# Gradient of wo: four 1 MB stores over 128 partitions against 64 stores over 8 partitions each

## Chip, cores and metric

The kernel runs on one core of one Trainium2 chip. The metric is the device time of one execution in microseconds (us): median of three runs 1698.76, from 1698.05 to 1699.05. The profile is of one further execution, taken by the hardware profiler. All engine times below are counted from the first instruction of that execution. PE is the matmul engine, ACT, DVE and POOL the other three compute engines, and SP the engine that only issues transfers here. Sixteen DMA engines move the data between HBM and the on-chip memory.

## What is computed

Forward and backward of one transformer block at decode: four batch rows, one new token each, width 512, 32 heads of 128, cached keys and values of 4096 positions per head, and a gated feed-forward layer of width 1792.

```python
def _A_ref(x, k_cache, v_cache, wq, wo):
    q = (x @ wq).reshape(B, Sq, H, Dh).transpose(0, 2, 1, 3)
    scores = jnp.einsum("bhqd,bhkd->bhqk", q, k_cache) * (Dh ** -0.5)
    p = _softmax(scores, axis=-1)
    o = jnp.einsum("bhqk,bhkd->bhqd", p, v_cache)
    return o.transpose(0, 2, 1, 3).reshape(B, Sq, H * Dh) @ wo
...
h = x + _A_ref(_layernorm(x, axis=-1), A_k_cache, A_v_cache, A_wq, A_wo)
h2 = h + _B_ref(_layernorm(h, axis=-1), B_w1, B_w3, B_w2)
```

The outputs are `h2` and the gradients of x, k_cache, v_cache, wq, wo, w1, w3 and w2, all bf16. The caches are 128 heads (batch times head) of 4096 x 128 each, 1 MB a head: K is read once, V twice, and both gradients, `out_2` for K and `out_3` for V, are written once. That is most of the 707 MB moved. The gradient of wo, `out_5`, is 4096 x 512: for every batch row an outer product of the attention output (4096 wide) and the gradient at the block's output (512 wide), summed over the four rows. It is 4 MB.

## The kernel before

The program is written with an explicit order of instructions for each engine (a manual schedule); a framework puts the semaphores between them. On-chip memory is one arena of 23 slots of some 8 KB per partition. `Slot` takes one slot, `Slot2` a pair of neighbours, and `give` returns it when the last user has been issued, not when it is done; the next user of the slot then waits on semaphores. Which free slot is taken follows from how long ago, in program order, each was given back.

The work goes in three stages. In the first, to about 650 us, K and V are read head by head, and scores, softmax and per-head sums are formed. The second, short, does the feed-forward layer. The third reads V again and writes the gradients of both caches. It begins one head at a time (`for s in range(SP)`, SP = 32 heads) and then goes over pairs of heads: `for t in range(NT)`, 48 passes, each with these steps in this order:

- `load_pairs(t + LP)` (L1280): SP issues the load of one 2 MB pair of V, some passes ahead;
- `front_pair(t + LP, ...)`: PE transposes the eight parts of a V pair (L1298), ACT copies them back (L1299), PE forms the products for dP (L1313). In its middle stands a call of `side`;
- `more_V`: DVE makes the 2 MB gradient of a V pair as an outer product (L1379), SP stores it to `out_3` (L1389). How far V's gradients run ahead of K's shrinks near the end, and a pass in which it shrinks makes none;
- `grad_pair(out_2, ...)`: the same two lines for the gradient of K; after every second pass `group_dS_pair` (L1326, L1329) prepares the next two;
- `side(s + 1)`.

`side` moves the small work forward: a generator, `side_work`, that holds everything which isn't a gradient of the caches. In this loop each call of `side` takes two steps, from one `yield` to the next, so a pass has four. A step is mostly one `grad_unit`: a matmul (L984) into one of two PSUM buffers named `gps`, and the copy by ACT of the unit before (L978). The last part of `side_work` is the gradient of wo, L1139 to L1148: four blocks of 1024 rows, each made of eight units in a slot over 128 partitions (eight rows of `out_5`, 8 KB, in each partition) and stored by one transfer on SP (L1146). After the last of them the flag `side_done` lets the pairs take any slots.

SP issues its transfers in program order and waits, before each, for what the transfer needs. Everything that moves in bulk goes through its one queue. At the end of the program SP waits for all transfers (L1519).

Of the kernel before, what the change touches and what calls it, by code (L numbers as in the profile page):

```python
# [27 lines left out]
def kernel(  # L28
# [22 lines left out]
    nc = tc.nc  # L51
    P = nc.NUM_PARTITIONS

    B = A_x.shape[0]
    D = A_x.shape[-1]
    H = A_k_cache.shape[1]
# [4 lines left out]
    HD = H * Dh  # L61
# [152 lines left out]
    def ones_window(col):  # L214
# [11 lines left out]
                          in_=rowg[:, None, :, None].to_broadcast([P, 4, 8, 4]))  # L226
# [70 lines left out]
    with ExitStack() as c0:  # L297
# [11 lines left out]
        for h in range(H):  # L309
            for cc in range(DC):  # L310
                nc.tensor.matmul(qT_ps[:, h, :], lhsT=wq_s[cc].b(HD)[:, h * Dh:(h + 1) * Dh], rhs=xhatT[:, cc, :],
                                 start=(cc == 0), stop=(cc == DC - 1))
# [4 lines left out]
        for r in range(2):  # L317
            for t_ in range(2):
                for q in range(4):
                    nc.tensor.matmul(qr_ps[32 * q:32 * (q + 1), 2 * r + t_, :], lhsT=ident_b[:, 64 * r + t_:64 * (r + 1):2],  # L320
                                     rhs=qT_bf[:], start=True, stop=True, tile_position=(0, 32 * q))
# [514 lines left out]
    with ExitStack() as cm:  # L836
# [33 lines left out]
        for wi, wt in enumerate((w1, w3)):  # L870
            for fc in range(FC):
                for cc in range(DC):
                    nc.tensor.matmul(gu_ps[:, wi, fc, :], lhsT=w13_view(wt, cc)[:, fc * P:(fc + 1) * P], rhs=hhatT[:, cc, :],  # L873
                                     start=(cc == 0), stop=(cc == DC - 1))
# [25 lines left out]
        for jj in range(DC):  # L900
            i_mm = 0
            for (lt, wt) in ((d_gateT_bf, w1), (d_upT_bf, w3)):
                for fc in range(FC):
                    nc.tensor.matmul(dn_ps[:, jj, :], lhsT=w13_view(wt, jj)[:, fc * P:(fc + 1) * P], rhs=lt[:, fc, :],  # L904
                                     start=(i_mm == 0), stop=(i_mm == 2 * FC - 1))
# [12 lines left out]
        ps = psA.tile([P, REP, Dh], FP32, tag="rT", name="repq_ps")  # L918
# [4 lines left out]
        for s in range(3):  # L923
# [8 lines left out]
                         start=True, stop=True)  # L932
# [14 lines left out]
        for b0, b1 in ((0, 1), (1, B)):  # L947
            ps = psA.tile([P, B, Dh], FP32, tag="rT", name="rep_ps")
            for b in range(b0, b1):
                for jj in range(DC):  # L950
                    nc.tensor.matmul(ps[:, b, :], lhsT=dhT[:, jj, b:b + 1].to_broadcast([P, P]), rhs=wo_page(0)[:, 0, jj, :],
                                     start=(jj == 0), stop=(jj == DC - 1))
# [12 lines left out]
    with ExitStack() as c2:  # L965
# [9 lines left out]
        def grad_flush():  # L975
            if gu:
                dst, ps, n = gu.pop()
                nc.scalar.copy(out=dst, in_=ps[:, 0:n])  # L978


        def grad_unit(dst, lhsT, rhs):
            n = rhs.shape[-1]
            ps = psg.tile([P, 512], FP32, tag="gps", name="gps")
            nc.tensor.matmul(ps[:, 0:n], lhsT=lhsT, rhs=rhs, start=True, stop=True)  # L984
            grad_flush()
            gu.append((dst, ps, n))

# [22 lines left out]
        def side_work():  # L1010
# [22 lines left out]
            for cc in range(DC):  # L1033
# [9 lines left out]
                for h in range(H):  # L1043
                    nc.tensor.matmul(dx_ps[0:B, cc * P:(cc + 1) * P], lhsT=dqT_bf[:, h * B:(h + 1) * B], rhs=wv[:, h, :],
                                     start=(h == 0), stop=(h == H - 1))
# [19 lines left out]
            for cc in range(DC):  # L1065
                st = Slot("gwq")
                for n8 in range(HD // 512):
                    grad_unit(st.b(HD)[:, n8 * 512:(n8 + 1) * 512], xhat_bf[0:B, cc * P:(cc + 1) * P],
                              flat.b(HD)[0:B, n8 * 512:(n8 + 1) * 512])
                    yield  # L1070
                grad_flush()
                nc.sync.dma_start(out=out_4[cc * P:(cc + 1) * P, :], in_=st.b(HD))
                if cc == DC - 1:
                    flat.give()
                    fs.give()
                st.give()
# [5 lines left out]
            gr_bf, dh_bf, hhat_bf = r1.t[0:B, 2 * F:2 * F + D], r2.t[0:B, F:F + D], r2.t[0:B, F + D:F + 2 * D]  # L1082
# [29 lines left out]
            for i in range(2):  # L1112
                st = Slot("gw2")
                hw = hh_rows[:, i * 7 * P:(i + 1) * 7 * P].rearrange("b (p k) -> b k p", k=7)
                for k in range(7):
                    grad_unit(st.b(7 * D)[:, k * D:(k + 1) * D], hw[:, k, :], gr_bf)
                    yield
                grad_flush()
                nc.sync.dma_start(out=out_8[i * 7 * P:(i + 1) * 7 * P, :].rearrange("(p c) j -> p c j", c=7),
                                  in_=st.b(7 * D).rearrange("p (c j) -> p c j", c=7))  # L1120
                st.give()
            oflat = Slot("oflat")
            for b in range(B):
                nc.gpsimd.dma_start(out=oflat.b(HD)[b:b + 1, :], in_=O_sb[b::B, :])
            for (rows, out_ap) in ((dg_rows, out_6), (du_rows, out_7)):
                for i in range(2):
                    st = Slot("gw13")
                    nw = hhat_bf[0:B, i * 2 * P:(i + 1) * 2 * P].rearrange("b (p k) -> b k p", k=2)
                    for k in range(2):
                        for (f0_, w_) in f_chunks:  # L1130
                            grad_unit(st.b(2 * F)[:, k * F + f0_:k * F + f0_ + w_],
                                      nw[:, k, :], rows[:, f0_:f0_ + w_])
                            yield
                    grad_flush()
                    nc.sync.dma_start(out=out_ap[i * 2 * P:(i + 1) * 2 * P, :].rearrange("(p c) f -> p c f", c=2),
                                      in_=st.b(2 * F).rearrange("p (c f) -> p c f", c=2))
                    st.give()
            r1.give()
            for h0 in range(0, H, 8):  # L1139
                st = Slot("gwo")  # L1140
                ow = oflat.b(HD)[0:B, h0 * P:(h0 + 8) * P].rearrange("b (p k) -> b k p", k=8)
                for k in range(8):
                    grad_unit(st.b(8 * D)[:, k * D:(k + 1) * D], ow[:, k, :], dh_bf)
                    yield
                grad_flush()
                nc.sync.dma_start(out=out_5[h0 * P:(h0 + 8) * P, :].rearrange("(p k) j -> p k j", k=8),  # L1146
                                  in_=st.b(8 * D).rearrange("p (k j) -> p k j", k=8))
                st.give()  # L1148
            oflat.give()
            r2.give()  # L1150
            part["side_done"] = True

        units["s"] = side_work()


# [368 lines left out]
```

## Time and profile before

| | |
|---|---|
| median of three runs | 1698.76 us |
| lowest and highest | 1698.05, 1699.05 us |
| span of the profiled execution, first to last instruction | 1696.2 us |
| median less that span | 2.6 us |
| busy: PE, DVE, ACT, POOL | 73%, 73%, 57%, 20% of the span |
| bytes moved by DMA | 707.45 MB, 417 GB/s over the span |
| SP's queue | 80416 packets, 704.94 MB |
| stores L1146 (gradient of wo) | 4 of 1 MB, issued from 1513.2 to 1610.4, landing 25.7 to 30.5 us later |
| stores L1389 (gradient pairs) | 96 of 2 MB, issued from 899.1 to 1666.8 |
| V pair loads L1280 | 48 of 2 MB, the last issued at 1610.8 |
| copies L978, 128x512 | 594 ns median |
| matmuls L984, four rows by 128 and 512 columns | 432 ns median |

The single execution that was profiled has no device time of its own beside its span; the table sets the span against the median. In the profile a row of slices gives the busy share in 40 equal parts of the span, one digit in tenths each. "Landing" is the time from the issue of a transfer to its last completion: each transfer reports 16 completions, and it has landed when all have come. In a list of waits, "A <- B" says that A waited for B, with the total in us, the number of times and the longest. In a timeline, a line gives the start and length of a run of like instructions, in us.

### The profile page before, as it was taken

The numbers are of one execution on the slowest core, as the hardware profiler recorded it, in microseconds if no ns is written. First come the engines' busy times: TensorE is split into PE (matmuls) and PEld (weight loads), VectorE is DVE, ScalarE is ACT, GpSimd is POOL, SyncE is SP. The second block draws the span as 40 slices with busy tenths as digits, with TensorE's granted clock in tenths as the row PEclk, the third lists the DMA queues.
The fourth block names the chain that finished last, engine by engine and source line by source line (L and its number), as shares of the span: only waits on it lengthen the run. The fifth ranks groups of instructions, "written<-read, shape, count | busy, mean of one in ns | idle before, by whom it ended". The sixth has DMA issues, their size and how long they took to land.

```text
span 1696.2 us, 37839 instructions
## 1 busy us (share of the span) xinstructions
PE 1233.4 (73%) x16228; PEld 943.4 (56%) x16228; DVE 1234.4 (73%) x1198; ACT 959.5 (57%) x1490; POOL 336.9 (20%) x583
## 2 busy tenths in 40 slices
PE   5889888888888888877876755667665666766650
PEld 4777667666677666655655544444444444444440
DVE  5989999999998997667766466575665655655683
ACT  3555544454454544677665555666665666666650
POOL 1211222222222222222231121011210102011120
PEclk8999999999999999899898689886678777676675
DMA  9999999999999999999999999999999999999995
GB/s 401 424 424 424 424 424 424 424 424 423 416 423 406 424 414 397 395 414 425 425 425 429 428 429 428 429 430 429 429 429 428 418 430 429 422 418 425 415 429 230
DMA packets 81000, 707.45 MB, mean 417 GB/s; under 512 B 8748, under 2 KB 12984, under 8 KB 15296
## 3 DMA queue, kind: packets, MB, share of 16 engines
q1 hardware_dynamic: 80416, 704.94, 99.0%
q8 instruction: 127, 2.08, 0.5%
q14 instruction: 41, 0.34, 0.0%
q0 software_dynamic: 416, 0.10, 0.0%
HBM read 422.59 MB, written 282.34 MB: 416 GB/s over the span
## 4 chain that ended last, share of the span: by engine, by line
DMA 46%; DVE 9%; PE 3%; issue 2%; ACT 1%; DVEq 0%; POOL 0%; SPq 0%; ACTq 0%
DMA out_dram<-arena 43%; DVE arena L1379 7%; DMA arena<-in_A_v_cache_dram 3%; DVE arena L806 1%; PE M_ps L472 1%; DVE arena L457 1%; PE pt_w L601 0%; ACT arena L1299 0%; ACT Pn L436 0%; DVEq L1519 0%; PE kP_ps L482 0%; DVE dPr L1326 0%; PE pt_tps L1298 0%; PE gu_ps L873 0%; PE dn_ps L904 0%
## 5 line engine op out<-in xcount | busy, mean ns | idle before, releaser
L1299 ACT COPY arena<-pt_tps 128x1024 bf16<-128x1024 bf16 x384 | 369.8, 1023 | 232.3 <-PE pt_tps L1298 231.6
L1298 PE MATMUL pt_tps<-ident_b,arena 128*128 128x128 bf16 x3072 | 308.1, 272 | 204.7 <-DMA arena<-in_A_v_cache_dram 149.4
L1298 PEld LDWEIGHTS <-arena 128*128 128x128 bf16 x3072 | 263.9, 125 | 304.2 <-DMA arena<-in_A_v_cache_dram 172.8
L1379 DVE TENSOR_TENSOR arena<-arena 128x8192 bf16<-128x8192 bf16 x48 | 212.5, 4427 | 205.1 <-DMA out_dram<-arena 202.3
L472 PE MATMUL M_ps<-arena 128*128 128x130 bf16 x4096 | 285.1, 222 | 42.9 <-DMA arena<-in_A_v_cache_dram 42.2
L457 DVE TENSOR_TENSOR arena<-arena 128x4096 bf16<-128x4096 bf16 x128 | 292.5, 2285 | 23.9 <-POOL arena L453 23.9
L472 PEld LDWEIGHTS <-arena 128*128 128x128 bf16 x4096 | 251.9, 99 | 64.0 <-DMA arena<-in_A_v_cache_dram 57.2
L1379 DVE TENSOR_TENSOR arena<-dS,arena 128x8192 bf16<-128x8192 bf16 x48 | 212.3, 4424 | 73.0 <-DMA out_dram<-arena 73.0
L364 DVE STREAM_TRANSPOSE arena<-arena 128x512 f32<-128x512 f32 (+1 forms) x321 | 250.7, 797 | 0.0
L359 ACT COPY arena<-pt_tps 128x1024 bf16<-128x1024 bf16 x128 | 129.5, 1012 | 188.9 <-PE pt_tps L358 150.5
L1376 POOL COPY arena<-arena 128x128 bf16<-128x128 bf16 x48 | 55.3, 1153 | 492.3 <-ACT arena L1353 286.3
L370 POOL TENSOR_TENSOR W<-qrep,wmask 128x128 bf16<-128x128 bf16 x128 | 120.2, 939 | 85.6 <-PE S_ps L390 70.8
L801 ACT COPY arena<-pt_tps 128x1024 bf16<-128x1024 bf16 x128 | 121.7, 1025 | 26.1 <-PE pt_tps L800 24.8
L453 POOL COPY arena<-P_all 128x64 bf16<-128x64 bf16 x128 | 32.7, 255 | 412.8 <-ACT P_all L447 409.8
L806 DVE TENSOR_TENSOR arena<-dS,arena 128x4096 bf16<-128x4096 bf16 x32 | 73.2, 2293 | 35.0 <-DMA out_dram<-arena 34.7
L800 PE MATMUL pt_tps<-ident_b,arena 128*128 128x128 bf16 x1024 | 78.5, 229 | 27.1 <-ACT arena L801 27.1
L1313 PE MATMUL dP_ps<-arena 128*32 128x512 bf16 x768 | 85.7, 484 | 7.6 <-ACT arena L1299 7.3
L800 PEld LDWEIGHTS <-arena 128*128 128x128 bf16 x1024 | 67.2, 104 | 37.5 <-issue 35.9
L447 ACT COPY P_all<-pt_P 32x64 bf16<-32x64 bf16 x256 | 52.1, 204 | 53.6 <-PE pt_P L443 51.4
L806 DVE TENSOR_TENSOR arena<-P,arena 128x4096 bf16<-128x4096 bf16 x29 | 66.4, 2295 | 19.8 <-DMA out_dram<-arena 19.8
L358 PE MATMUL pt_tps<-ident_b,arena 128*128 128x128 bf16 x1024 | 80.1, 222 | 0.0
L482 PE MATMUL kP_ps<-arena,onesw 128*32 128x512 bf16 x1024 | 79.6, 388 | 0.0
(245 smaller groups left out, 1576.5 us busy)
## 6 DMA issues: line engine op xcount, KB each, us to landing
out_dram<-arena SPq DMA_DIRECT2D x96, 2048.0 KB, 27.9
arena<-in_A_v_cache_dram SPq DMA_DIRECT2D x160, 1024.0 KB, 15.9
arena<-in_A_k_cache_dram SPq DMA_DIRECT2D x128, 1024.0 KB, 15.3
arena<-in_A_v_cache_dram SPq DMA_DIRECT2D x48, 2048.0 KB, 32.1
out_dram<-arena SPq DMA_DIRECT2D x72, 1024.0 KB, 20.2
arena<-in_A_wq_dram SPq DMA_DIRECT2D x8, 1024.0 KB, 14.4
arena<-in_B_w_dram SPq DMA_DIRECT2D x8, 896.0 KB, 15.3
out_dram<-arena SPq DMA_DIRECT2D x6, 896.0 KB, 28.4
```

The lines of the kernel that those rows point to most:

```text
L359: nc.scalar.copy(out=KT[:, c * GW:(c + 1) * GW, :], in_=pt[:])
L364: nc.vector.transpose(out=KT[:, c * w_:(c + n) * w_], in_=Kn[:, c * w_:(c + n) * w_])
L370: nc.gpsimd.tensor_tensor(out=W[:, hl], in0=qrep[:, :, s:s + 1].to_broadcast([P, 4, 32]), in1=wmask[:, hl, None, :].to_broadcast([P, 4, 32 ...
L457: nc.vector.tensor_tensor(out=PK[:, :, 0:Dh].rearrange("p j (r t) -> p j r t", t=2), in0=Ks[s].heads().rearrange("p j (r t) -> p j r t", t=2),
L472: nc.tensor.matmul(hold["M"][:], lhsT=Vn[:, j, :], rhs=PK[:, j, :], start=(j == 0), stop=(j == SJ - 1))
L800: nc.tensor.transpose(pt[:, i, :], v[:, g * GW + i, :], ident_b[:])
L801: nc.scalar.copy(out=v[:, g * GW:(g + 1) * GW, :], in_=pt[:])
L806: nc.vector.tensor_tensor(out=dst.rearrange("p j (r t) -> p j r t", t=2), in0=col2[:, :, None, :].to_broadcast([P, SJ, Dh // 2, 2]), in1=r ...
L1298: nc.tensor.transpose(pt[:, i, :], v[:, g * GW + i, :], ident_b[:])
L1299: nc.scalar.copy(out=v[:, g * GW:(g + 1) * GW, :], in_=pt[:])
L1313: nc.tensor.matmul(rows["acc"][32 * c:32 * (c + 1), :], lhsT=zt[t % B][:, 32 - m:64 - m], rhs=v[:, j0:j0 + 4, :], start=(pl == 0 and u == ...
L1379: nc.vector.tensor_tensor(out=dst.rearrange("p (j r t) -> p j r t", r=Dh // 2, t=2), in0=col2[:, :, None, :].to_broadcast([P, 2 * SJ, Dh / ...
```

## The change

The gradient of wo is made in eight blocks of 512 rows instead of four of 1024. A block lies on partitions 0 to 63 only, each still holding eight rows of `out_5` (8 KB). It still takes eight units, of half the output partitions, now two to a step, so that a block takes four steps and the whole part 32, as before. A block is stored by eight transfers on SP instead of one: each takes eight partitions that are 4 apart (0, 4, ..., 28, then 1, 5, ..., 29, and so on, and the same from 32), 64 KB in eight pieces of 8 KB. In all there are 64 transfers in the place of four, and 64 matmuls and copies in the place of 32. The matmul and the copy of `grad_unit` now write and read only as many partitions as their destination has; for the other gradients that is all 128 as before.

```diff
 def grad_flush():
     if gu:
         dst, ps, n = gu.pop()
-        nc.scalar.copy(out=dst, in_=ps[:, 0:n])
+        nc.scalar.copy(out=dst, in_=ps[0:dst.shape[0], 0:n])
 ...
-    nc.tensor.matmul(ps[:, 0:n], lhsT=lhsT, rhs=rhs, start=True, stop=True)
+    nc.tensor.matmul(ps[0:dst.shape[0], 0:n], lhsT=lhsT, rhs=rhs, start=True, stop=True)
 ...
-for h0 in range(0, H, 8):
+for h0 in range(0, H, 4):
     st = Slot("gwo")
-    ow = oflat.b(HD)[0:B, h0 * P:(h0 + 8) * P].rearrange("b (p k) -> b k p", k=8)
+    ow = oflat.b(HD)[0:B, h0 * P:(h0 + 4) * P].rearrange("b (p k) -> b k p", k=8)
     for k in range(8):
-        grad_unit(st.b(8 * D)[:, k * D:(k + 1) * D], ow[:, k, :], dh_bf)
-        yield
+        grad_unit(st.b(8 * D)[0:64, k * D:(k + 1) * D], ow[:, k, :], dh_bf)
+        if k % 2:
+            yield
     grad_flush()
-    nc.sync.dma_start(out=out_5[h0 * P:(h0 + 8) * P, :].rearrange("(p k) j -> p k j", k=8),
-                      in_=st.b(8 * D).rearrange("p (k j) -> p k j", k=8))
+    rows_ = out_5[h0 * P:(h0 + 4) * P, :].rearrange("(p k) j -> p (k j)", k=8)
+    for b0 in (0, 32):
+        for o in range(b0, b0 + 4):
+            nc.sync.dma_start(out=rows_[o:o + 29:4, :], in_=st.b(8 * D)[o:o + 29:4, :])
     st.give()
```

## Prediction

> **What bounds the kernel now.** I read the page first: slices, DMA queues and DMA issues.
>
> ```profile
> DMA  9999999999999999999999999999999999999995
> q1 hardware_dynamic: 80416, 704.94, 99.0%
> q8 instruction: 127, 2.08, 0.5%
> out_dram<-arena SPq DMA_DIRECT2D x96, 2048.0 KB, 27.9
> ```
>
> The DMA engines are busy from end to end, nearly all of it for SP's queue; no compute engine is over 73%. A 2 MB store lands 27.9 us after its issue, although 2 MB at the stage's 428 GB/s take 4.9 us: about six transfers lie in the queue at once. Next, the busy shares by stretch, of the last microseconds (columns: us, then PE, PEld, DVE, ACT and POOL busy, clock, DMA share, GB/s).
>
> ```profile
> 1660.00:1674.00 14.00, 0.00 (x0) 0.00 (x0) 6.79 (x2) 0.00 (x0) 0.00 (x0) 0.50 1.01 432
> 1677.00:1694.00 17.00, 0.00 (x0) 0.00 (x0) 0.00 (x0) 0.00 (x0) 0.00 (x0) 0.50 0.06 27
> ```
>
> Until 1674 all 16 engines work at 432 GB/s, 27 each. From 1677 on the share is 0.06 = 1/16, at 27 GB/s: one engine still works off some 18 us, with everything else done. One engine is behind all others and ends the run, at 1694.9 (the last store, issued at 1666.8, lands 28.1 us later). The median engine's completion of each transfer, which the trace's semaphore updates give, shows the same: the last of 16 is 5 us behind the eighth around 890, 12 us around 1210, 18 us from 1530 on.
>
> Then SP's own timeline at the start, where no buffer has yet been used twice, and its waits there (us in total, times, longest).
>
> ```profile
> 0.74 2.10 SPq L171 DMA_DIRECT2D arena<-in_A_wq_dram  x4
> 2.89 2.01 SPq L178 DMA_DIRECT2D arena<-in_A_k_cache_dram  x4
> 5.57 8.26 SPq L178 DMA_DIRECT2D arena<-in_A_k_cache_dram  x4
> SPq L178 <- DMA arena<-in_A_wq_dram: 7.6, 4, 2.7
> ```
>
> Eight transfers go out in 4.9 us. The ninth, a K load into a slot that nothing has touched, waits for a wq load, and leaves at 5.57, when the first (issued at 0.74, landing 4.8 later) has landed. SP has eight completion semaphores and goes round them; a transfer is issued only when the one eight places before it has landed on all its engines. Over the 530 issues of the trace none leaves earlier than that, and 82 leave within 0.3 us of it. Around the change this costs nothing, since six are in flight:
>
> ```profile
> 1563.19 0.33 SPq L1389 DMA_DIRECT2D out_dram<-arena  x1
> 1563.61 0.66 SPq L1280 DMA_DIRECT2D arena<-in_A_v_cache_dram  x1
> 1573.14 5.31 SPq L1389 DMA_DIRECT2D out_dram<-arena  x2
> 1578.68 0.50 SPq L1146 DMA_DIRECT2D out_dram<-arena  x1
> 1579.26 1.16 SPq L1280 DMA_DIRECT2D arena<-in_A_v_cache_dram  x1
> ```
>
> This is two passes of the t loop in SP's order: V load, store of out_3, store of out_2, V load, two stores, the wo store (L1146), V load. Each wo store sits between the last gradient store of one pass and the V load of the next.
>
> **The change, part by part.** *Compute.* 32 more matmuls (432 ns median) and 32 more copies (594 ns for 128x512; 64 partitions have as many elements each, so the same by estimate): 14 us of PE and 19 us of ACT over eight passes, 2.4 us of ACT a pass. In 1497 to 1611, seven passes, ACT runs 78 of 114 us and L1299 alone waits 30.9 us for PE, which waits for V loads. Cost nothing; without that cover at most 19 us. The yields stay 32, so no other step moves; the eight blocks end one per pass, the first at 1497 instead of 1513.
>
> *Bytes.* Still 4 MB. Eight rows cannot feed sixteen engines alike. With one row to an engine, eight engines get 64 rows of 8 KB, where each of the sixteen now gets 32. 32 rows x 8 KB at 27 GB/s = 9.7 us more on eight engines and 9.7 less on the others. From both sides: the late engine gains 9.7 us, or loses it.
>
> The Trainium skill ("DMA: Bandwidth & Descriptors", "Why a DMA increments its semaphore by 16 and not by 1") says that a transfer whose outer dimension is 8 runs on the eight lowest engines, and the same page ("Latency and other measured facts") says engines 7 and 15 are usually slower than the rest; no row here numbers the late engine. If it were 15, these rules alone would make the time 1698.76 - 9.7 = 1689; if 7, 1708.5.
>
> *SP's order.* This decides. In each pass SP now has V, A (out_3), B (out_2) and eight small stores w1 to w8, then the next V: 11 transfers round 8 semaphores. w6 needs this pass's V landed, w7 needs A, and w8 needs B, issued directly before w1. Behind w8 in SP's queue stand the next V load and all gradient stores. So once a pass SP stops until everything large has landed on the last engine; the queue of six runs dry and starts again. The next V itself needs only w1, which is in the rings right behind B.
>
> One restart costs what the first load shows: issue to landing 4.8 us for 1 MB, of which 1 MB at 428 GB/s is 2.45, leaves 2.4; w8's issue (0.33) and two semaphore steps (0.05 each) make 2.8. On top, all 16 engines must be done, not the average one: instruction fetches (0.5% of 16 engines' time over 127 packets, 1.07 us each, one per 13 us) fall on one engine in most passes, for which I add 0.7, an estimate. 3.5 us. Its ends: 2.4 (w8 free, no unevenness), and 5.0 (a gradient store not ready when SP wakes: DVE needs 4.43 us each, so half of one).
>
> Is DVE ready? Two products and the dS steps take 10.5 us of a pass of some 18, and a pair of slots is reused two passes later, when its store has landed. DVE works ahead while SP stands. Taken as ready.
>
> *The sum, on the profiled run.* B of the first block's pass is issued at 1497.2 and lands 29.0 later: 1526.2, unchanged. SP's queue holds 24 L1389 stores and 8 V loads after it, 32 transfers of 2 MB at 4.9 us = 156.8. Eight restarts x 3.5 = 28.0. Last landing 1711.0; the span ends 1.3 after it as now (1696.2 - 1694.9): 1712.3, 16.1 more. Span and median differ by 2.6 (1698.76 - 1696.2): 1698.76 + 16.1 = **1714.9 us**. The wo bytes are no term any more: w1 to w7, some 2.1 us on their engines, run in the gap between B's data and the next V's data, which is why it matters little whether the late engine carries them. The same accounting of before, 1526.2 + 156.8 + 4 x 2.45 for the wo stores, gives 1692.8 where 1694.9 was measured: it is good to some 2 us. With 2.4 and 5.0 a restart: 1706.1 and 1726.9.
>
> The skill's rule against this change ("DMA: Bandwidth & Descriptors", "Rules for kernel authors": coalesce, since small transfers are mostly overhead; its fit has a fixed 2 us per transfer) would make 60 more transfers 120 us if each stood alone. No run here shows 64 KB stores; the rows show transfers overlapping in the rings, so I do not use it.
>
> **The rivals.** *Faster: only the bytes count.* If SP is not held by the transfer eight places before (the small stores' semaphores taken outside the round, or early completions counted), the queue stays full and the late engine, if it is one of the eight relieved, ends 9.7 us sooner: 1689. It decides if a w8 leaves while B is in flight. For it: one engine alone ends the run. Against it: the L178 wait above.
>
> *Bytes count, on the wrong side.* No drain, and the late engine is one of the eight loaded: 1698.8 + 9.7 = 1708.5.
>
> *Drain and starved producers.* SP's stop also delays what feeds DVE (slots, V loads), so that each of the seven later passes waits for one whole product: 7 x 4.43 = 31 more, 1746. For it: DVE already waits for landed stores, 50.9 us in 1497 to 1611. Against: those waits end as soon as the queue drains.
>
> *It does not do what it says:* each small store is split over all engines. The eight at once remain, so the drain too; w1 to w7 add half as much to each engine inside the gap. 1713 to 1717, not told apart by the time.
>
> **How the numbers follow.** Drain with ready producers 0.83 (with the split case in it); only the bytes, faster, 0.07; only the bytes, slower, 0.04; starved producers 0.06. Predicted is the likeliest, 1715. Range 1706 to 1727: the restart's two ends; it also holds the loaded-side rival. About 0.2% (3.4 us) is what a measurement of this kernel can tell from no change. Faster 0.06, within 0.2% 0.03 (the late engine's gain and a cheap drain cancelling), slower 0.91.
>
> **What would show it.** Right: in the changed profile, SP's waits between 1500 and 1660 name the small stores' line waiting for out_dram and V-load transfers, some 10 us or more a pass; the timeline shows V, A, B bunched within 2 us, then none for the rest of an 18 us pass; the DMA share falls from 1.0 to some 0.8 to 0.9 in that stretch; 2 MB landings there fall below 20 us; the lone engine's tail at the end shrinks to a few us, its lead having been given back in the first drain. Wrong: small stores issued in one burst without waits, DMA share 1.0, and an end moved by 10 us either way (the bytes); or V, A, B spread apart by DVE waits (starved producers).

## The result and the profile after

| | before | after |
|---|---|---|
| median of five runs each, beside each other | 1698.32 us | 1724.77 us |
| lowest and highest | 1697.02, 1699.05 | 1722.98, 1725.9 |
| span of the profiled execution | 1696.2 | 1723.0 |

The ratio is 1.0156, with a 95% interval of 1.0143 to 1.0168: 26.4 us slower. Forecast was 1715, so slower by 16 to 17, in the range 1706 to 1727. The direction and the place were right; 10 us are missing from the sum, and the runs show that one of its steps was wrong, not only a size.

First the page of after, the same two rows as before (DMA share by slice, SP's queue), and the count of its packets.

```profile
DMA  9999999999999999999999999999999999958889
DMA packets 81449, 707.46 MB, mean 411 GB/s; under 512 B 9196, under 2 KB 13432, under 8 KB 15744
q1 hardware_dynamic: 80864, 704.94, 97.8%
```

The hole is in slices 36 to 39, which is 1508 to 1680. The last slice is now full, where it was half empty. The packets are 448 more, all of them under 512 B (8748 before): 64 stores with eight completions each, less four with sixteen, is 448. The semaphore updates agree: each small store has one about a microsecond after its issue and eight more as its data land, not sixteen. So each small store ran on eight engines, and the rival in which it is split over all of them is out.

The busy shares by stretch of after: before the change sets in, in the t loop, and at the end (columns as before: us, then the busy time of PE, PEld, DVE, ACT and POOL, clock, DMA share, GB/s).

```profile
1480.00:1497.00 17.00, 12.15 (x93) 7.92 (x92) 10.13 (x8) 10.80 (x17) 5.02 (x4) 0.60 1.00 421
1500.00:1660.00 160.00, 112.94 (x854) 76.46 (x846) 63.76 (x33) 105.68 (x143) 53.33 (x13) 0.63 0.77 310
1704.00:1722.00 18.00, 0.00 (x0) 0.00 (x0) 8.98 (x3) 0.00 (x0) 0.00 (x0) 0.50 0.93 394
```

In the same 160 us the kernel before moves 424 GB/s at a share of 1.01:

```profile
1500.00:1660.00 160.00, 97.63 (x892) 67.56 (x891) 108.07 (x53) 97.27 (x121) 20.90 (x15) 0.72 1.01 424
```

The share falls to 0.77, below the 0.8 to 0.9 that was forecast. In the last 18 us all engines work: the lone engine's tail is gone, as forecast.

SP's timeline of after, from the first small stores on (start, length of the run of like instructions, line):

```profile
1503.00 23.36 SPq L1150 DMA_DIRECT2D out_dram<-arena  x8
1526.47 0.38 SPq L1283 DMA_DIRECT2D arena<-in_A_v_cache_dram  x1
1533.09 4.76 SPq L1392 DMA_DIRECT2D out_dram<-arena  x2
1537.95 8.90 SPq L1150 DMA_DIRECT2D out_dram<-arena  x8
1546.96 0.38 SPq L1283 DMA_DIRECT2D arena<-in_A_v_cache_dram  x1
1552.78 4.76 SPq L1392 DMA_DIRECT2D out_dram<-arena  x2
1557.71 8.82 SPq L1150 DMA_DIRECT2D out_dram<-arena  x8
```

The first eight small stores take 23 us, and w8 leaves at 1525.74, when the semaphore updates show B landed on the last engine at 1525.72 (forecast 1526.2). That is the round of eight as predicted. After that the picture is another one: V, A and B are not bunched within 2 us. A leaves 6 us behind V, and B 4.4 behind A. The eight small stores then take 8.8 us, about 1.1 each. The waits say who holds whom. First SP's own, from 1500 to 1660 (us in total, times, longest):

```profile
SPq L1392 <- DVE arena L1382: 63.8, 13, 6.2
SPq L1150 <- DMA out_dram<-arena: 15.3, 6, 4.4
SPq L1150 <- DMA arena<-in_A_v_cache_dram: 4.2, 1, 4.2
```

Then those of DVE and POOL, from 1526 to 1660:

```profile
POOL arena L1379 <- DMA out_dram<-arena: 108.0, 6, 39.6
DVE arena L1382 <- DMA out_dram<-arena: 90.1, 7, 30.9
```

SP waits three times as long for DVE's products as for landings (63.8 against 19.5), and of the 19.5 only some 1.5 come after the first drain. DVE waits for stores. DVE's own timeline shows which (in brackets the idle time before, and what ended it):

```profile
1528.64 4.42 DVE L1382 TENSOR_TENSOR arena<-arena 128x8192 bf16<-128x8192 bf16 x1 [30.90 <-DMA out_dram<-arena]
1548.32 4.42 DVE L1382 TENSOR_TENSOR arena<-arena 128x8192 bf16<-128x8192 bf16 x1 [9.16 <-DMA out_dram<-arena]
1568.31 4.43 DVE L1382 TENSOR_TENSOR arena<-arena 128x8192 bf16<-128x8192 bf16 x1 [11.13 <-DMA out_dram<-arena]
1587.52 4.43 DVE L1382 TENSOR_TENSOR arena<-arena 128x8192 bf16<-128x8192 bf16 x1 [8.69 <-DMA out_dram<-arena]
```

The last small store of each block, w8, lands at 1528.32, 1548.24, 1567.94 and 1587.30: each time DVE starts 0.1 to 0.4 us later. The instruction streams hold the reason: the framework puts a wait for all eight stores of the block in front of the next product (L1382) and in front of POOL's copy for it (L1379), as if a transfer over every fourth partition touched the whole arena. The product does not need that wait: stores of adjacent partitions, with all else the same (adjacent8, below), get none.

One whole pass can now be added up, from the V load at 1586.02 to the next at 1605.09. w8 before it is issued at 1585.29 and lands 2.0 later; DVE starts 0.2 after that; its product takes 4.4 and A leaves at 1591.97; B, from the second, leaves 4.4 later, at 1596.40; w1 to w8 leave from 1596.83 to 1604.37, V 0.7 later. B has landed at 1603.38, a microsecond before w8 leaves. In this pass nothing waits for the round of eight; in three of the seven (those that begin at 1526.5, 1547.0 and 1624.1) w8 leaves within 0.02 us of B's landing, and the round decides.

### The profile page after: what moved, and what is told of

It reads as the page before. It is cut to its first block, busy times and chain, and to the rows that moved or that the text cites. A ratio compares the mean times of both kernels' runs of the same rounds, so it can differ in the third digit from the quotient of the medians.

```text
span 1723.0 us, 38071 instructions
## 1 busy us (share of the span) xinstructions
PE 1260.8 (73%) x16260; PEld 965.0 (56%) x16260; DVE 1234.2 (72%) x1198; ACT 976.6 (57%) x1522; POOL 397.0 (23%) x583
## 3 DMA queue, kind: packets, MB, share of 16 engines
q8 instruction: 127, 2.08, 0.5%
## 4 chain that ended last, share of the span: by engine, by line
DMA 38%; DVE 10%; ACT 3%; issue 3%; PE 2%; SPq 2%; DVEq 0%; ACTq 0%
DMA out_dram<-arena 36%; DVE arena L1382 9%; ACT arena L801 3%; SPq L1150 2%; DMA arena<-in_A_v_cache_dram 1%; DVE arena L806 1%; PE dq_ps L1000 1%; PE pt_tps L800 1%; PE dP_ps L1231 1%; PE pt_wo L610 0%; DVEq L1522 0%; DVE dPr L1329 0%; PE rep_ps L1182 0%; ACT dPr L1206 0%; PE dOT_ps L773 0%
## 5 line engine op out<-in xcount | busy, mean ns | idle before, releaser
L1301 PE MATMUL pt_tps<-ident_b,arena 128*128 128x128 bf16 x3072 | 319.2, 278 | 196.2 <-DMA arena<-in_A_v_cache_dram 139.0
L1301 PEld LDWEIGHTS <-arena 128*128 128x128 bf16 x3072 | 274.3, 128 | 289.2 <-DMA arena<-in_A_v_cache_dram 160.3
L1382 DVE TENSOR_TENSOR arena<-arena 128x8192 bf16<-128x8192 bf16 x48 | 212.5, 4428 | 264.0 <-DMA out_dram<-arena 261.8
L472 PEld LDWEIGHTS <-arena 128*128 128x128 bf16 x4096 | 253.6, 99 | 55.2 <-DMA arena<-in_A_v_cache_dram 48.8
L1382 DVE TENSOR_TENSOR arena<-dS,arena 128x8192 bf16<-128x8192 bf16 x48 | 212.9, 4436 | 59.2 <-DMA out_dram<-arena 59.2
L1379 POOL COPY arena<-arena 128x128 bf16<-128x128 bf16 x48 | 88.5, 1845 | 524.1 <-ACT arena L1356 224.8
L800 PE MATMUL pt_tps<-ident_b,arena 128*128 128x128 bf16 x1024 | 78.7, 230 | 27.1 <-ACT arena L801 27.1
L984 PE MATMUL gps<-arena 4*128 4x512 bf16 (+2 forms) x142 | 63.4, 469 | 43.2 <-ACT arena L978 42.4
L800 PEld LDWEIGHTS <-arena 128*128 128x128 bf16 x1024 | 67.3, 105 | 37.5 <-issue 36.0
L1316 PE MATMUL dP_ps<-arena 128*32 128x512 bf16 x768 | 81.0, 451 | 9.4 <-ACT arena L1302 9.1
L978 ACT CAST arena<-gps 128x512 bf16<-128x512 f32 (+2 forms) x142 | 76.1, 579 | 19.0 <-PE gps L984 10.9
L1293 POOL COPY arena<-dOT_bf 128x2 bf16<-128x2 bf16 x48 | 70.0, 1463 | 59.0 <-PE dP_ps L1316 59.0
```

The lines of the kernel that those rows point to most:

```text
L472: nc.tensor.matmul(hold["M"][:], lhsT=Vn[:, j, :], rhs=PK[:, j, :], start=(j == 0), stop=(j == SJ - 1))
L800: nc.tensor.transpose(pt[:, i, :], v[:, g * GW + i, :], ident_b[:])
L1301: nc.tensor.transpose(pt[:, i, :], v[:, g * GW + i, :], ident_b[:])
L1379: nc.gpsimd.tensor_copy(out=pP2[t], in_=P_two(t, 1)[:, 0, :, None].to_broadcast([P, 2 * SJ, 2]))
L1382: nc.vector.tensor_tensor(out=dst.rearrange("p (j r t) -> p j r t", r=Dh // 2, t=2), in0=col2[:, :, None, :].to_broadcast([P, 2 * SJ, Dh / ...
```

## The experiments

Theory at the outset: the round of eight drains the queue (as predicted), and DVE's wait for the strided stores adds to it. Rivals: one of the two alone; the small size itself; the added compute; the late engine's bytes. Times are medians; the kernel before, run in between, had 1698.23, 1697.79, 1697.91 and 1697.72 in the four groups.

**adjacent8: the stride taken away, the count kept.**

```diff
-for b0 in (0, 32):
-    for o in range(b0, b0 + 4):
-        nc.sync.dma_start(out=rows_[o:o + 29:4, :], in_=st.b(8 * D)[o:o + 29:4, :])
+for o in range(0, 64, 8):
+    nc.sync.dma_start(out=rows_[o:o + 8, :], in_=st.b(8 * D)[o:o + 8, :])
```

> As the changed kernel, but each of the eight small stores of a block takes eight adjacent partitions instead of eight that are 4 apart: again 64 stores of 64 KB in the same places of SP's queue. The one thing that goes is a wait in the program: only with the strided stores do DVE's gradient products (L1382) and POOL's copies (L1379) wait for all eight small stores of the block before. Theory (the drain, and on top of it DVE held by the small stores): the drain stays, DVE is ready when SP wakes, passes take some 18.1 us instead of 19.5, and the time is 1714 to 1716, some 10 us below the changed kernel. Rival (the drain alone with dearer restarts, or 0.65 us and more per small issue on SP): no change from the changed kernel, 1723 to 1727. Rival (the bytes on eight engines and the half-filled partitions): no change either.

1727.39 us, ratio 1.0177 (1.0160 to 1.0194): no faster than the change. The theory's 1714 to 1716 missed; it is the rival's result (the drain alone, with dearer restarts), 0.4 above its range. Its SP timeline is the picture that the prediction drew:

```profile
1546.65 0.36 SPq L1282 DMA_DIRECT2D arena<-in_A_v_cache_dram  x1
1547.12 0.84 SPq L1391 DMA_DIRECT2D out_dram<-arena  x2
1548.19 18.09 SPq L1149 DMA_DIRECT2D out_dram<-arena  x8
1566.38 0.36 SPq L1282 DMA_DIRECT2D arena<-in_A_v_cache_dram  x1
```

V, A and B leave within 1 us; in the run of 18 us w6 leaves at 1555.33, w7 at 1560.20 and w8 at 1566.01, and V, A and B have landed on the last engine at 1555.32, 1560.18 and 1565.99. So DVE's wait isn't needed for a pass of 19.7 us: SP's waits for landings give it without that wait (from 1500 to 1660 its engines move 307 GB/s at a share of 0.82). The restart also costs more than the 3.5 that was forecast. V lands on the median engine 8.2 us after its issue, where 4.9 of bytes and 2.4 of start had been put; the last engine has B 1.3 behind the median, for which 0.7 had been added; w8 and V's place behind it take 0.4. With two more transfers of 4.9 that makes the 19.7. Over the seven passes (1526.86 to 1660.63, 133.8 us, of which 98 are 20 transfers of 4.9) a restart costs 5.1.

**every_second: two strided stores a block, five transfers in a pass.**

```diff
-for b0 in (0, 32):
-    for o in range(b0, b0 + 4):
-        nc.sync.dma_start(out=rows_[o:o + 29:4, :], in_=st.b(8 * D)[o:o + 29:4, :])
+for o in range(2):
+    nc.sync.dma_start(out=rows_[o:o + 63:2, :], in_=st.b(8 * D)[o:o + 63:2, :])
```

> As the changed kernel, but each block of 64 partitions goes out in two stores of every second partition (32 rows each, 256 KB) instead of eight: five transfers a pass, so SP's round of eight semaphores never empties the queue; but DVE and POOL still wait for both stores of the block before, since these are strided too. All 16 engines share the bytes. Theory (DVE held by strided stores is a cause by itself): DVE cannot start a pass's products until the last block's stores have landed, the DMA engines idle some 2 us a pass, passes of some 18 us, 1708 to 1714. Rival (only the round of eight semaphores costs): 1698 to 1701, as the kernel before.

1717.53, ratio 1.0114 (1.0098 to 1.0129). Here the round does not hold: from 1526 to 1660 no transfer leaves within 0.3 us of the landing eight places before. So the rival that knew only the round is out. DVE's line, in its waits (1526 to 1660) and then in its timeline:

```profile
DVE arena L1381 <- DMA out_dram<-arena: 93.2, 8, 30.8
```

```profile
1547.73 4.42 DVE L1381 TENSOR_TENSOR arena<-arena 128x8192 bf16<-128x8192 bf16 x1 [8.36 <-DMA out_dram<-arena]
```

The second of the two stores had landed at 1547.61. The loss is larger than expected, though (1708 to 1714); its controls follow (one_store, two_halves32).

**one_store: one store a block.**

```diff
-for b0 in (0, 32):
-    for o in range(b0, b0 + 4):
-        nc.sync.dma_start(out=rows_[o:o + 29:4, :], in_=st.b(8 * D)[o:o + 29:4, :])
+nc.sync.dma_start(out=rows_, in_=st.b(8 * D)[0:64, :])
```

> As the changed kernel, but each block of 64 partitions is stored by one transfer of 512 KB: four transfers a pass, no strided store, 16 engines. What stays of the change: eight blocks on partitions 0 to 63, twice the matmuls and copies, and a wait of the block's copies on ACT for the store of the block before. Theory (only the small strided stores cost): 1698 to 1704, the upper end if ACT's wait for a store 28 us in flight holds the transposes. Rival (the half-filled partitions and the doubled PE and ACT work cost): 1710 or more.

1707.23, ratio 1.0052 (1.0037 to 1.0067): between the two expectations. Neither the round (one transfer of 32 from 1526 to 1660 leaves within 0.3 us of the landing eight places before) nor DVE's wait for a small store is here, and 9 us are left. Against it every_second, with DVE's wait and without the round too, is 10.3 us slower. The lone engine ends the run again, and the semaphore updates show it slow at these stores: from the second block to the seventh it needs 2.43, 2.10, 2.08, 1.91, 1.55 and 3.29 us for a store of 512 KB that takes 1.2 to 1.3 at its own rate. Together that is 5.6 of the 9 us; the rest lies in its loads and gradient stores.

**seven: 119 partitions a block, on seven engines.** 119 partitions can be shared out evenly to seven engines only; the trace shows seven completions of the transfer, beside one update half a microsecond after the issue.

```diff
+rows_ = out_5.rearrange("(p k) j -> p (k j)", k=8)
+for p0 in range(0, 512, 119):
+    n_ = min(119, 512 - p0)
...
+    nc.sync.dma_start(out=rows_[p0:p0 + n_, :], in_=st.b(8 * D)[0:n_, :])
```

> As the kernel before, with the gradient of wo in four blocks of 119 partitions and one of 36, one store each. 119 rows divide over 7 engines at most, 36 over 12, so 476 of the 512 rows of 8 KB should go to seven engines (39 rows or 11.9 us more each), and the others lose 29 rows or more (8.8 us). In the changed kernel the first small store, on eight engines, lands 0.3 us after the last engine has finished the large store before it, while seven of its eight completions are 16 us earlier: the late engine is one of the eight loaded ones. Theory (the late engine sets the end, and is the eighth of these eight): it is relieved, the seven others have 20 us to spare, 1689 to 1692, 8 us faster than before. Rival (late engine among the seven): 1708 to 1711. Rival (the order of completion does not set the end): 1697 to 1701.

1717.03, ratio 1.0112 (1.0097 to 1.0127). The hope to relieve the late engine falls: it is one of the seven. Its 17 rows a store take it 5.4 to 7.2 us (5.2 at 27 GB/s), and the five stores together 25.8 where the four before took 10.1: 15.7 of the 19 us lost. The time is so above the rival's 1708 to 1711 too. The late engine ends alone:

```profile
1700.00:1715.00 15.00, 0.00 (x0) 0.00 (x0) 0.00 (x0) 0.00 (x0) 0.00 (x0) 0.50 0.06 24
```

**halves, doubled: what in one_store costs 9 us.** Both start from the kernel before. halves cuts its store in two, doubled makes each unit twice.

```diff
-nc.sync.dma_start(out=out_5[h0 * P:(h0 + 8) * P, :].rearrange("(p k) j -> p k j", k=8),
-                  in_=st.b(8 * D).rearrange("p (k j) -> p k j", k=8))
+for o in (0, 64):
+    nc.sync.dma_start(out=rows_[o:o + 64, :], in_=st.b(8 * D)[o:o + 64, :])
```

```diff
-grad_unit(st.b(8 * D)[:, k * D:(k + 1) * D], ow[:, k, :], dh_bf)
+for _ in range(2):
+    grad_unit(st.b(8 * D)[:, k * D:(k + 1) * D], ow[:, k, :], dh_bf)
```

> The kernel before, whose wo store of 128 partitions (1 MB, four times) is cut into two stores of 64 adjacent partitions (0 to 63, then 64 to 127, 512 KB each). Compute as before: 32 matmuls, 32 copies. With one_store the DMA engines were busy (share 0.98) but moved 394 GB/s instead of 424, and its 512 KB stores took the late engine some 2.1 us each where 1.25 is a full-rate share. Theory (a transfer that touches only 64 adjacent partitions moves at a lower rate): eight such stores again, so 7 to 10 us more than before, 1705 to 1709, with the same lower rate. Rivals (the cost of one_store is the doubled matmuls and copies, or ScalarE's wait for the store of the block before): neither is here, so 1697 to 1701.

> The kernel before with each of the 32 matmuls of the wo gradient and each of their copies made twice, into the same place (the second overwrites the first with the same values); stores as before. This is the added compute of the change alone: 32 matmuls and 32 copies, 14 us of PE and 19 us of ACT. Theory, and the step of the prediction that costs it at nothing: 1697 to 1701. Rival (ACT or PE work reaches the path): up to 19 us more, 1705 to 1717.

halves: 1700.29, ratio 1.0017 (1.0007 to 1.0026). doubled: 1697.76, ratio 1.0001 (0.9991 to 1.0010). The 32 added matmuls and copies cost nothing, as the prediction had it. halves is where its rivals put it, at their upper end: a store of 64 partitions is not slow whenever it comes. But neither rival is the cause: doubled takes away the compute, and eight128, below, ScalarE's wait.

**two_halves32, four16: the control for the stride, and the count.**

```diff
-for b0 in (0, 32):
-    for o in range(b0, b0 + 4):
-        nc.sync.dma_start(out=rows_[o:o + 29:4, :], in_=st.b(8 * D)[o:o + 29:4, :])
+for o in (0, 32):                                # four16: range(0, 64, 16)
+    nc.sync.dma_start(out=rows_[o:o + 32, :], in_=st.b(8 * D)[o:o + 32, :])   # o + 16
```

> The changed kernel with two stores a block, of partitions 0 to 31 and 32 to 63 (256 KB each): five transfers in a pass, so the round of eight does not close on its own pass, and, the partitions being adjacent, neither VectorE nor GpSimd waits for them. every_second has the same number and size of stores, on the same 64 partitions, but strided, with that wait, and took 1717.5. Theory (VectorE's wait for the strided stores costs every_second some 10 us beside the bytes): 1704 to 1711, at most 4 above one_store's 1707.2, without VectorE waits for out_dram just after a small store lands. Rival (two stores of 256 KB are dear by their number or size): 1715 to 1720.

> The changed kernel with four stores a block, of 16 adjacent partitions each (128 KB): seven transfers in a pass, one fewer than the eight semaphores, so no small store waits for its own pass's V load, A or B. adjacent8, with eleven, took 1727.4. Theory (the round of eight is what costs adjacent8, and it bites only when a pass has more than eight transfers): 1704 to 1712, no drain, SP's V loads some 15 to 16 us apart. Rival (the cost grows with the number of small stores, each a fixed price): between one_store's 1707 at one and adjacent8's 1727 at eight, 1715 to 1718.

two_halves32: 1706.68, ratio 1.0054 (1.0039 to 1.0069), the same as one_store. Against it every_second, with the same stores and bytes in strided form, is 10.8 us slower, and DVE waits 55.4 us for stores in 1526 to 1660 instead of 93.2:

```profile
DVE arena L1381 <- DMA out_dram<-arena: 55.4, 12, 8.5
```

With the 10.3 over one_store, that prices the stride at some 10 us. DVE's hold is the wait that it adds, and the DMA share from 1500 to 1660 falls with it from 0.98 to 0.83. But the strided stores are also slower by themselves: from 1526 to 1660 a packet of 8 KB (one row of one partition) takes 0.63 us at the median, where it takes 0.31 in the other kernels (in after too, with every fourth partition), and these packets fill 16.1 us of each engine's time instead of 11.1. So up to 5 of the 10 us can be theirs; the runs do not split them from the hold.

As a control two_halves32 is less clean than it was meant to be. With five transfers in a pass the round does hold SP, 19 times from 1526 to 1660, as one of its waits (from 1500 on) shows:

```profile
SPq L1282 <- DMA out_dram<-arena: 23.5, 6, 4.7
```

That costs little, since the engines stay busy. On the late engine its small stores lose only 2.4 us, where one_store's lose 5.6, so that the two times agree does not mean that the time is lost in the same place.

four16: 1714.39, ratio 1.0096 (1.0081 to 1.0112). The theory as I had written it, that a pass with seven transfers pays nothing to the round, missed, and the rival (a fixed price for each small store) by 0.6 us only. Against a fixed price stands that twice the stores cost nothing from one_store to two_halves32. SP does wait for the round:

```profile
SPq L1149 <- DMA out_dram<-arena: 45.0, 11, 5.3
SPq L1391 <- DMA out_dram<-arena: 33.5, 7, 5.6
SPq L1391 <- DMA arena<-in_A_v_cache_dram: 14.2, 7, 4.4
```

With seven in a pass, the transfer eight places before is of the pass before: A waits for the last V, B for the last A, w1 for the last B. The late engine is that far behind: A leaves at 1549.74 (V landed 1549.68), B at 1554.99 (1554.92), w1 at 1560.65 (1560.58). SP can be only eight transfers ahead of the slowest engine, and four of those are small, so the round can hold SP with fewer than eight transfers in a pass. But the engines hardly run dry meanwhile:

```profile
1500.00:1660.00 160.00, 106.17 (x875) 74.83 (x871) 93.90 (x45) 106.94 (x145) 12.52 (x16) 0.72 0.96 360
```

Against the kernel before, the share falls by a twentieth and the rate by 15%: the larger part of the loss is that the packets became slower. From 1526 to 1660 one of 8 KB takes 0.52 us on the mean where it took 0.32 before, and one of 16 KB 0.68 instead of 0.62.

**eight128, pool_queue: the blocks, and the round on SP.** eight128 makes eight blocks with one store each like one_store, but on 128 partitions with four rows each. pool_queue is adjacent8 with the small stores issued by GpSimd, whose queue has semaphores of its own.

```diff
-for h0 in range(0, H, 8):
+for h0 in range(0, H, 4):
...
-ow = oflat.b(HD)[0:B, h0 * P:(h0 + 8) * P].rearrange("b (p k) -> b k p", k=8)
-for k in range(8):
+ow = oflat.b(HD)[0:B, h0 * P:(h0 + 4) * P].rearrange("b (p k) -> b k p", k=4)
+for k in range(4):
...
+nc.sync.dma_start(out=out_5[h0 * P:(h0 + 4) * P, :].rearrange("(p k) j -> p (k j)", k=4),
+                  in_=st.b(8 * D)[:, 0:4 * D])
```

```diff
-    nc.sync.dma_start(out=rows_[o:o + 8, :], in_=st.b(8 * D)[o:o + 8, :])
+    nc.gpsimd.dma_start(out=rows_[o:o + 8, :], in_=st.b(8 * D)[o:o + 8, :])
```

> Eight blocks as in the change, one store of 512 KB each, but on all 128 partitions with four rows of wo in each (4 KB per partition) instead of 64 partitions with eight: 32 matmuls and 32 copies of 128x512, eight staging buffers taken instead of four, four transfers in a pass. one_store has the same blocks, stores and bytes on 64 partitions and took 1707.2; there ScalarE stood 9.7 us at the second block's first copy, for a staging buffer whose last store was still under way. Theory A (the blocks come twice as often, so the second finds no free staging buffer, SP stands behind it and the queue runs dry): 1704 to 1708, with ScalarE's wait of 8 to 10 us again. Theory B (64 partitions are slower to read): 1697 to 1700, though the wait is there.

> adjacent8 (eight stores of eight adjacent partitions a block, 1727.4) with the small stores issued from GpSimd's queue instead of SP's. That queue has completion semaphores of its own, so SP again has three transfers in a pass and its V loads and gradient stores wait for no small store; number, size and partitions of the stores are the same. Theory (the round of eight on SP is what adjacent8 pays above one_store's 1707): 1704 to 1711, without bunched V, A, B on SP. Rival (64 stores of 64 KB are dear by their number, wherever issued): 1720 to 1735.

eight128: 1697.49, ratio 0.9999 (0.9990 to 1.0009). Eight blocks with eight stores are free; theory A there, the staging buffer, falls, though ScalarE's wait is there (6.6 us). pool_queue: 1719.45, ratio 1.0128 (1.0113 to 1.0143): 8 us of adjacent8's loss go, V, A and B are no longer bunched, and no transfer of SP's leaves within 0.3 us of the landing eight places before, but it stays 8 us above the theory's range and only 0.6 below the rival's. So the round on SP is not all that the eight small stores cost. What is left shows at its end, here and in the loop of eight128 for comparison:

```profile
1702.00:1716.00 14.00, 0.00 (x0) 0.00 (x0) 0.00 (x0) 0.00 (x0) 0.00 (x0) 0.50 0.06 27
```

```profile
1500.00:1660.00 160.00, 93.31 (x880) 65.02 (x877) 107.08 (x53) 96.33 (x120) 16.41 (x15) 0.76 1.00 421
```

In pool_queue one engine is last again: the fifteenth has the last store at 1699.5, the sixteenth at 1716.5. From the first B's landing there (1529.2) it takes 187.3 us; 32 transfers at 4.9 leave 30.5. If it gets one row of 8 KB of each small store here too, which no run shows (a store from GpSimd's queue reports sixteen completions), its 64 rows would be 19.4 at 27 GB/s. That would be the prediction's second rival, bytes on the wrong side, which comes out once the round is taken away; 11 us stay unexplained, beside that its 8 KB packets too are slower, 0.43 us on the mean from 1526 to 1660.

**straddle, packed64: which 64 partitions.** Both make each block on 128 partitions and store 64 of them; straddle takes 32 to 95 in six blocks of eight, packed64 0 to 63 and 64 to 127 by turns. They differ in one line:

```diff
+p0 = min(max(64 * j - 32, 0), 512 - P)    # packed64: 64 * (j - j % 2)
+o = 64 * j - p0
...
+nc.sync.dma_start(out=rows_[64 * j:64 * j + 64, :], in_=st.b(8 * D)[o:o + 64, :])
```

> Eight blocks, each made on all 128 partitions (64 matmuls and 64 copies of 128x512, as in doubled, which cost nothing), of which one store of 64 partitions leaves: of partitions 32 to 95 in six blocks, of 0 to 63 in the first and of 64 to 127 in the last. Bytes, number and size of the stores and partitions in each are one_store's (1707.2); only which 64 is new. Theory A (what one_store pays is how few of the memory's ports its partitions reach; the Trainium skill's page on SBUF puts 0 to 63 and 64 to 127 on eight ports each, 32 to 95 on sixteen): 1697 to 1701. Theory B (64 partitions, whichever, are slower than 128): 1705 to 1709.

> The control for straddle: the same 64 matmuls and copies, and one store of 64 partitions a block, of 0 to 63 in four blocks and of 64 to 127 in the other four, by turns. Theory A (ports) and theory B (64 partitions): one_store's loss again, 1703 to 1709, unless taking turns between the two halves spares the late engine, since the others are about one pass ahead of it and then use the other half's ports: 1698 to 1702.

straddle: 1700.79, ratio 1.0019 (1.0009 to 1.0028), two thirds of one_store's 9 us gone. packed64: 1702.70, ratio 1.0026 (1.0014 to 1.0038), nearly half of them gone. In the stores nothing but the choice of partitions differs from one_store. On the late engine a store takes 1.25 to 1.58 us in straddle and 1.20 to 1.56 in packed64, against up to 3.3 in one_store. In one_store the late engine is about one pass behind the others, so that it reads a block's partitions while they begin to read the same ones for the next block: its store from 1579.5 to 1581.6 meets theirs, which land from 1580.7 on, and so it is with those of 2.10 and 1.91. In straddle and packed64 the two are of different partitions. That 64 partitions are slow when all engines want the same ones at once fits this, but the slowest store, 3.29 us, does not meet another, so it is argued and not shown.

Not only the late engine is slower. From 1500 to 1660 the engines are busy nearly all the time in these kernels (share 0.96 to 1.01), but they move 424 GB/s before, 421 in eight128, 412 in halves, 403 in straddle, 399 in packed64, 394 in one_store, 381 in two_halves32 and 360 in four16. So the rate falls with the partitions that a small store takes at a time, 128, 64, 32 and 16, though these stores are few of the bytes; why, the runs do not show.

The Trainium skill ("SBUF — State Buffer", "Door 1: The DMA port swizzle") says that partitions 0 to 63 reach only eight of the sixteen ports to the DMA engines, no more than 0 to 31, and 0 to 127 all sixteen. The runs agree in part of the order: 0 to 63 in one store cost 9 us, all 128 nothing (eight128), and 32 to 95, which by that map reach all sixteen, a third. But packed64 and halves, whose stores reach eight ports each, cost only 5.0 and 2.5 us, so the number of ports that a store reaches does not set the price by itself. That straddle keeps 3 us is not explained; two of its eight stores are still of one half.

## Why the prediction was right, and where it was wrong

*Right in the first drain: SP's order decides, by the eight semaphores.* The first drain came when forecast (1525.7 for 1526.2), and adjacent8 and four16 show SP leaving within 0.1 us of the landing eight places before. The tail after the last drain, from the V load at 1659.0 to the last landing at 1721.9, is 62.9 us, where the sum of twelve transfers at 4.9 and a restart of 3.5 gives 62.3. The span ends 1.1 later. All of the 10 us missing are therefore in the seven passes between: 132.5 us from 1526.5 to 1659.0, where the sum has 20 transfers of 4.9 and seven restarts of 3.5, 122.5. The restart came to (132.5 - 98) / 7 = 4.9. But in these passes SP waits only some 1.5 us for landings, and what came is the sign that the prediction named for being wrong: V, A and B spread apart by DVE's waits. That the time still lies in the range is partly luck. adjacent8, which has the predicted mechanism without DVE's hold, took 1727.4, just outside.

*Wrong: "Taken as ready".* The step failed on DVE. It assumed that DVE works ahead while SP stands; instead DVE was held in every pass until the last small store had landed, a wait that the change itself adds through its stride. The prediction asked who waits for the small stores only of SP's queue, and not of DVE and POOL. With w8 a pass's last transfer, the two products come after everything else, and SP finds A 6 us late. The rival "starved producers" had the right engine with another cause (slots and V loads) and charged 31 us on top, as if the delays added. every_second prices the stride at some 10 us where the round does not hold, the slower packets of its stores included.

*Wrong: the cost of w's issue, 0.33 us.* The strided small store takes SP 0.655 us (median), and the eight from w1 to the next V 8.3 us:

```profile
L1150 SPq DMA_DIRECT2D out_dram<-arena x64: 625/655/1375, 1503.0 to 1658.3; - x64
```

In four of seven passes this, not B's landing, is what the next V waits for. Adjacent stores take 0.293 (adjacent8).

*Mis-sized: the restart itself.* Even with DVE free and cheap issues it is 5.1 instead of 3.5 (adjacent8): the stated upper end, but for other reasons than the half product given there. In the pass shown above, 0.9 of that is V's landing and 0.6 the last engine. Why a 2 MB load into a dry queue needs 8.2 us there, where 4.8 for 1 MB at the start gives 7.3, is left open; in after, where A and B are not queued right behind it, it needs 7.2.

*Not additive.* The stride costs some 10 us (every_second), 64 small stores on SP 20.2 (adjacent8 over one_store; 8 of them go when GpSimd issues them), and the 64 partitions 9 (one_store). Together they cost 26.4, not 39: the hold and the round both end in a dry queue, and where the hold delays A and B, the round has less left to wait for.

*Right: compute at nothing* (doubled; ACT's 78 of 114 us is the sum of its lines, the engine was busy for 75.6), *eight blocks at nothing* (eight128), *the bytes no term while the queue drains.* w1 to w8 of a block land on the late engine 0.3 us apart (1526.05 to 1528.32 for the first block), its full rate for 8 KB. Without the drain they would be a term, and on the wrong side, as pool_queue suggests. The late engine is one of the eight that the small stores use: w1 of the first block is on seven engines by 1510.0 and on the last at 1526.05, just behind B. The late engine also is among seven's seven.

## What to carry to other kernels

When a change splits or strides a transfer, read in the instruction stream which other engines got a wait for it: here such a wait of a producer, with the slower packets of the strided stores, cost some 10 us (every_second). Look up which transfer lies eight places before each one in the same queue: where it is one of the same pass, SP stands until that has landed on the slowest engine, and the others run dry (adjacent8). Where one engine is behind, price every store by what it does to that engine: how many rows it gets, and from which partitions (here 32 to 95 did better than 0 to 63, for a reason that is not settled).

## What the runs showed of the hardware beyond that

- One of the 16 DMA engines is 18 us behind from 1530 on in the kernel before, and it is among the seven that a transfer over 119 partitions uses and the eight that one over 8 uses.
- The Trainium skill ("DMA: Bandwidth & Descriptors", "Latency and other measured facts") names 7 and 15 as the usually slower engines; if, as the same page has it ("Why a DMA increments its semaphore by 16 and not by 1"), the lowest ones are used, the one here is none of those two.
- Eight partitions 4 apart take SP 0.655 us to issue, eight adjacent ones 0.293, and GpSimd 0.518 in pool_queue.
- The 8 KB packets of stores over every second partition took 0.63 us at the median (every_second), those of the other kernels 0.31.
- The same 512 KB of 64 partitions took the late engine 1.2 us or up to 3.3, in one_store, and at most 1.58 in straddle and packed64.
